# Larger projection sessions at block borders in an attention and mixture-of-experts kernel on one core

## The chip, the core and the metric

The kernel runs on one core of one Trainium2 chip. A core has five engines that run their own instruction streams and wait for each other by semaphores: TensorE (PE in the profile; its weight loads are shown apart as PEld), VectorE (DVE), ScalarE (ACT), GpSimd (POOL) and SyncE (SP, which here only issues DMAs). TensorE writes to PSUM, which has 8 banks of 512 fp32 columns on 128 partitions; DVE and ACT read PSUM and write SBUF. The metric is the device time of one execution in microseconds (us), the median of several runs. Lower is better.

## What is computed

```python
def _attn_ref(x, state):                 # x (8,8,512,64), state (8,8,32,64)
    scores = scale * x @ state^T         # every token against 32 states
    xread  = softmax(scores) @ state
    scores2 = scale * state @ x^T
    sread  = softmax(scores2) @ x
    return concat([xread, sread], axis=2)

def _moe_ref(x, w_gate, w1, w2):         # x (4352, 512), 8 experts, F = 1024
    P = exp(x @ w_gate - max); 8 rounds of row and column normalisation
    for e in range(E):
        out += P[:, e:e+1] * (maximum(x @ w1[e], 0) @ w2[e])
```

The rows of the second part are, for each of 8 batches, the 512 token rows of xread and the 32 state rows of sread, with 8 heads of 64 side by side.

## The kernel before

The first 141 us hold the attention, the gate with its normalisation rounds and expert 0. They are ordered by a small planner (`issue`, `op`) and are not touched by the change, apart from a variable that is dropped. The rest, experts 1 to 7, is written out by one loop (L871 to L894), and its order of issue is the order of execution on each engine.

The loop runs over (e, bi): expert e, and block bi of 9. Blocks 0 to 7 are the 512 token rows of a batch; block 8 (`bi == B`) is the **state block**, the 256 state rows of all batches. For each (e, bi) two layers are needed, and layer 1 of the next block is interleaved with layer 2 of this one.

**The projection** (`project`, L192 to L208). Since xread is softmax times state, x @ w1 is computed as softmax times (state @ w1). V = state @ w1 of one block is a tile of 2 pair groups by 1024 columns, made in two **halves** of 512 columns. A half is 8 small matmuls with 64 rows and 32 columns of the array each (`tile_position`), into two PSUM banks (q = 0, 1), and two ACT copies from them to V. A run of such matmuls without others between them is called a **session** here. Before, a session makes both halves of block work[i + 2], right after the first product of block i, and takes four banks of the pool with tag "h". State blocks have no projection, so the sessions stand in blocks 0 to 5, 7 and 8 of an expert. There are three V tiles.

**Layer 1** (`layer1`, L227 to L249) makes the hidden rows. One step makes one of 8 **hidden groups**: matmuls into a bank `hps` of pool "h" (4 banks in turn; two matmuls of 512 columns for a token block, four of 256 for the state block), and a relu on ACT into `Hm`. After the 4th and the 8th step DVE makes a set of four sums and differences from four relu results (L245 to L248, tile `sm` and a part of `Hm` in place). They are for the fast multiplication scheme with 7 products instead of 8.

**Layer 2** (`layer2`, L279 to L342) has the 7 **products**, k = 0 to 6. Each is 8 matmuls of 256 columns (4 in the state block) into one bank: A, E, B, A, B, E, B, where A and E are pools of one bank and B is one of two seed banks `Bseed`, used in turn by block number. After product 0 ACT copies A to the B bank, so that the further products add to it. After each of the products 1 to 6 DVE adds the bank, weighted by the routing column, to `acc` in two instructions (L307; one in the state block). A product into a bank waits for the add that read it.

**The interleaving** (L880 to L887). After product k follow so many steps of layer 1 as the pattern (0, 0, 1, 2, 2, 2, 1) says for k. `step()` is called after every product and every step of layer 1, 15 times a block; each sixth call advances the weight loader `load_w` (L160), which first issues the four weight DMAs of the next expert on POOL's queue, later makes eight DVE subtractions from w2 (tile `T`, L178). What is left of it is done at the end of block 6 (L891). In expert 1 POOL also scales `acc` by the first routing column (`weigh`, L251).

The last block has its own second layer (`layer2_last`).

Of the kernel before, what the change touches and what calls it, by code (L numbers as in the profile page):

```python
# [9 lines left out]
FP32 = mybir.dt.float32  # L10
FP16 = mybir.dt.float16
AX_X = mybir.AxisListType.X
ALU = mybir.AluOpType
AF = mybir.ActivationFunctionType
EPS = 1e-9


class Ring:
# [71 lines left out]
def kernel(  # L90
# [9 lines left out]
    nc = tc.nc  # L100

    B, H, S, D = x.shape
    Ns = state.shape[2]
    Dm, E = moe_w_gate.shape
    F = moe_w1.shape[2]
# [7 lines left out]
    NQ = NP // 2  # L113
# [19 lines left out]
    def bank(shape, dtype, name, tag="bank"):  # L133
        return pools[tag].tile(shape, dtype, name=name, tag=tag)
# [23 lines left out]
    vpool = ctx.enter_context(tc.tile_pool(name="vpool", bufs=3))  # L158
# [24 lines left out]
    w16 = [None] * E  # L183
# [5 lines left out]
    asb = actx.enter_context(tc.tile_pool(name="attn_sb", bufs=2))  # L189
    spl = actx.enter_context(tc.tile_pool(name="stprep", bufs=1))  # L190

    def project(e, bi):  # L192
        if bi == B:
            return
        w1h = w16[e][0]
        V = vpool.tile([128, NQ, F], FP16, name="V", tag="V")
        vt[(e, bi)] = V
        for f in range(F // 512):
            cols = ds(f * 512, 512)
            ps = [bank([128, 512], FP32, "v_ps", ring[0]) for _ in range(NQ)]  # L200
            for j in range(4):
                for q in range(NQ):
                    r = ((j ^ q) % 2) * 64
                    nc.tensor.matmul(ps[q][ds(j * Ns, Ns), :], stT[ds(r, 64), bi, q, ds((j ^ q) * Ns, Ns)],  # L204
                                     w1h[ds(r, 64), 2 * q + j // 2, cols],
                                     tile_position=(r, j * Ns))
            for q in range(NQ):
                nc.scalar.copy(out=V[:, q, cols], in_=ps[q])  # L208

    def hidden_ps(e, bi, fb, out):  # L210
        w1h = w16[e][0]
# [7 lines left out]
            nc.tensor.matmul(out, lhs, rhs, start=(k == 0), stop=(k == len(terms) - 1))  # L219

    vt = {}
    ring = ["bank"]
    hid = {}
    final = (E - 1, B)
    seeds = []

    def layer1(e, bi):  # L227

        t0, tn = blocks[bi]
        th = tn // 2  # L230
        Hm = hpool.tile([128, 2, NJ, S], FP16, name="Hm", tag="Hm")
        sm = hpool.tile([128, 3, NJ, S // 2], FP16, name="sm", tag="sm")
        hid[(e, bi)] = (Hm, sm)
        for j in range(NJ):
            for i in range(2):
                fb = i * NJ + j
                hps = bank([128, S], FP32, "hps", "h")
                hidden_ps(e, bi, fb, hps[:, :tn])
                nc.scalar.activation(out=Hm[:, i, j, :tn], in_=hps[:, :tn], func=AF.Relu)  # L239
                if j % 2 and i and (e, bi) != final:  # L240
                    jj = ds(j - 1, 2)
                    a11, a21 = Hm[:, 0, jj, :th], Hm[:, 0, jj, th:tn]
                    a12, a22 = Hm[:, 1, jj, :th], Hm[:, 1, jj, th:tn]
                    s1, s2, s4 = (sm[:, k, jj, :th] for k in range(3))
                    nc.vector.tensor_add(s1, a21, a22)  # L245
                    nc.vector.tensor_sub(a21, a11, a21)  # L246
                    nc.vector.tensor_sub(s2, s1, a11)  # L247
                    nc.vector.tensor_sub(s4, a12, s2)  # L248
                yield  # L249

    def weigh(b):  # L251
# [27 lines left out]
    def layer2(e, bi, n):  # L279
        t0, tn = blocks[bi]  # L280
        nk = tn // 256
        th = tn // 2
        Hm, sm = hid.pop((e, bi))
        w2h, T = w16[e][1], tsum[e]
        tb = t0 // 128
        p = Pmat[:, :, e:e + 1]
        A = bank([128, 2, DH], FP32, "A", "A")
        Eb = bank([128, 2, DH], FP32, "E", "E")

        def product(dst, lhs, rhs, first=False):  # L290
            for c in range(nk):
                for j in range(NJ):
                    nc.tensor.matmul(dst[:, c], lhs(j, c), rhs[:, j],  # L293
                                     start=first and c == 0 and j == 0, stop=(j == NJ - 1),
                                     skip_group_check=True)

        def h(i, half):
            return lambda j, c: Hm[:, i, j, ds(half * th + c * 128, 128)]

        def s(k):  # L300
            return lambda j, c: sm[:, k, j, ds(c * 128, 128)]

        def add(src, row, col):
            for c in range(nk):
                k = tb + row * nk + c
                dst = acc[:, k, ds(col * DH, DH)]
                nc.vector.scalar_tensor_tensor(out=dst, in0=src[:, c], scalar=p[:, k], in1=dst,  # L307
                                               op0=ALU.mult, op1=ALU.add)

        if e == 1:  # L310
            for b in range(2) if bi == 0 else (bi + 1,):
                weigh(b)
        product(A, h(0, 0), w2h[:, :NJ, :DH], True)
        if not n:
            for i in range(2):
                bb = pb.tile([128, 2, DH], FP32, name="Bseed%d" % i)
                nc.tensor.matmul(bb.rearrange("p c d -> p (c d)"), identh, aT[:, 0, 0], start=True, stop=True)
                seeds.append(bb)
        Bb = seeds[n % 2]
        nc.scalar.copy(out=Bb[:, :nk], in_=A[:, :nk])  # L320
        yield
        product(Eb, s(0), T[:, 0], True)
        add(Eb, 1, 1)
        yield
        product(Bb, s(1), T[:, 1])
        add(Bb, 0, 1)
        yield
        product(A, h(1, 0), w2h[:, NJ:, :DH])
        add(A, 0, 0)
        yield  # L330
        product(Bb, h(0, 1), T[:, 2])
        add(Bb, 1, 1)
        yield
        product(Eb, s(2), w2h[:, NJ:, DH:])
        add(Eb, 0, 1)
        yield
        product(Bb, h(1, 1), T[:, 3])
        add(Bb, 1, 0)
        if e == E - 1 and bi < B:
            for k in range(2 * nk):  # L340
                nc.sync.dma_start(out=outx[bi][:, k, :], in_=acc[:, tb + k, :])
        yield  # L342
# [44 lines left out]
    for g in range(2):  # L387
# [10 lines left out]
        out=wg_st, in_=moe_w_gate.rearrange("(kc p) e -> p kc e", p=128)))  # L398
# [28 lines left out]
    for g in range(4):  # L427
        ps = psum([128, 4, 128], FP16, "stT_ps")
# [13 lines left out]
    def gmul(_):  # L442
        for b in range(B):
            for j in range(4):
                for q in range(NQ):
# [6 lines left out]
                  lambda eng, q=q: copy(eng, G[:, :, q], gps[q].tile), [gm_op], uses=[gps[q]])  # L452
# [33 lines left out]
    for b in range(B):  # L486
        xT = slot(axt, 3, [128, H * NSC // 2, 128], FP16, "xT")
        xt_ready = []
        for g in range(2 if b < NT else 0):
            ps = psum([128, 8, 128], FP16, "xT_ps")  # L490
# [19 lines left out]
        for q in range(NQ):  # L510
            r = lambda n, b=b, q=q: (due_x(2 * b + q) + 0.1 * 5.54 * n,)
            ps = Slot(rings["pair"], lambda: bank([128, 2, 512], FP32, "psB", "pair"))
# [69 lines left out]
            s1 = op(r(4), {"DVE": (0.60, 0.80)}, subA, [m1], [], [eA, mxA])  # L582
# [71 lines left out]
    def tile_of(tag, shape):  # L654
# [4 lines left out]
    c = sk({"DVE": (0.36, 0.48)}, lambda: nc.vector.reduce_max(  # L659
        out=tile_of("lmx", [128, 1]), in_=logits.rearrange("p t e -> p (t e)"), axis=AX_X), gates)  # L660
    mT = psum([1, 128], FP32, "mT_ps")
    c = sk({"PE": (0.11, 0.35)}, lambda: nc.tensor.transpose(mT.tile, sm_["lmx"], ident32), [c, make32], takes=[mT])
    c = sk({"DVE": (0.25, 0.40)}, lambda: nc.vector.tensor_reduce(
        out=tile_of("gm", [1, 1]), in_=mT.tile, op=ALU.max, axis=AX_X, negate=True), [c], uses=[mT])
# [77 lines left out]
    for bi in range(len(blocks)):  # L742
        t0, tn = blocks[bi]
# [64 lines left out]
    for bi in range(2):  # L808
# [14 lines left out]
        for j in range(NJ):  # L823
# [11 lines left out]
            if j % 2:  # L835
                def sums(_, bi=bi, jj=ds(j - 1, 2), th=th, tn=tn):
                    Hm, sm = hid[1, bi]
                    a11, a21 = Hm[:, 0, jj, :th], Hm[:, 0, jj, th:tn]
                    a12, a22 = Hm[:, 1, jj, :th], Hm[:, 1, jj, th:tn]
                    s1, s2, s4 = (sm[:, k, jj, :th] for k in range(3))  # L840
                    nc.vector.tensor_add(s1, a21, a22)
                    nc.vector.tensor_sub(a21, a11, a21)
                    nc.vector.tensor_sub(s2, s1, a11)
                    nc.vector.tensor_sub(s4, a12, s2)
# [11 lines left out]
    for tag in ("A", "E"):  # L856
        pools[tag] = ctx.enter_context(
            tc.tile_pool(name="psum_" + tag, bufs=1, space=bass.MemoryType.PSUM))
    ring[0] = "h"
    n = 0  # L860

    def step():
# [6 lines left out]
                wload.pop(0)  # L869

    work = [(e, bi) for e in range(1, E) for bi in range(len(blocks))]  # L871
    for i, (e, bi) in enumerate(work):
        if bi == 1 and e + 1 < E:
            wload.append(load_w(e + 1))
        if (e, bi) == final:
            layer2_last()
            break
        l2 = layer2(e, bi, i)
        l1 = layer1(*work[i + 1]) if i + 1 < len(work) and work[i + 1] not in hid else iter(())
        for k in range(7):  # L880
            next(l2)
            step()
            if k == 0 and i + 2 < len(work) and work[i + 2] not in vt:
                project(*work[i + 2])
            for _ in range((0, 0, 1, 2, 2, 2, 1)[k]):
                next(l1, None)
                step()  # L887
        for part in (l1, l2):
            for _ in part:
                pass  # L890
        if bi == len(blocks) - 3:  # L891
            for _ in (x for w in wload for x in w):
                pass
            wload.clear()  # L894
# [30 lines left out]
```

## Time and profile before

| | |
|---|---|
| median of three runs | 766.16 us (766.08 to 768.02) |
| the profiled execution | 765.04 us |
| its span in the trace | 763.3 us |
| instructions | 16286 |
| experts 1 to 7, first product to last hidden group | 141.98 to 755.66 us |
| projection matmuls in them (L204) | 864, in 54 sessions |
| relu of layer 1 on ACT (L239) | 496, 572 ns each |
| copies of V on ACT (L208) | 216, 608 ns each |
| adds to acc on DVE (L307) | 708, 478 ns each |

A row of a view has the engine, the line of the kernel, the operation, the tile written and the tiles read, the shape and the count, then times in us. In a time line the first number is the start from the beginning of the span, the second the duration from the first start to the last end of the merged instructions; in square brackets stands how long the engine had been idle and which engine's work ended that. Consecutive matmuls overlap in these rows, since each is shown until its result is written: what a group costs is read from one start to the next.

### The profile page before, as it was taken

To read this page: it belongs to the slowest core of one execution; us is meant where nothing else is said; L and a number is where in the kernel's file an instruction comes from. 1 tells how busy PE (TensorE), PEld (TensorE's weight loads), DVE (VectorE), ACT (ScalarE), POOL (GpSimd) and SP (SyncE) were. 2 spreads that over 40 slices of the span, in tenths; PEclk is the share of its full clock that TensorE was granted. 3 is DMA by queue.
4 is the path that set the end of the run, shared out by engine and by line. 5 is a ranking of instruction groups with operands and counts; after the bars stand their busy time and mean duration, and the time that the engine had idled before them with its cause. 6 is when DMAs were issued, how large, how long until landed. Compare 5 with 4: busy or idle time off the path is not lost.

```text
span 763.3 us, 16286 instructions
## 1 busy us (share of the span) xinstructions
PE 747.2 (98%) x6557; PEld 501.5 (66%) x6557; DVE 626.8 (82%) x1533; ACT 513.3 (67%) x1002; POOL 104.5 (14%) x102
## 2 busy tenths in 40 slices
PE   5999999999999999999999999999999999999997
PEld 3444445566776667766776666766677666767676
DVE  6998977888987888888897888888887888878885
ACT  5888976666667675766657665676656666576652
POOL 4433100799200000100001000000001000000000
PEclk9999999999999999999999999999999999999999
DMA  8997200060015000510006000240006000002334
GB/s 135 190 147 123 46 1 1 1 112 1 1 24 89 1 2 1 88 25 2 1 1 111 2 1 1 38 75 1 1 2 101 11 2 1 1 34 85 104 111 139
DMA packets 41595, 34.61 MB, mean 45 GB/s; under 512 B 16688, under 2 KB 33072, under 8 KB 41520
## 3 DMA queue, kind: packets, MB, share of 16 engines
q0 software_dynamic: 21248, 20.97, 17.7%
q1 hardware_dynamic: 19040, 12.08, 6.0%
q8 instruction: 51, 0.84, 0.5%
q10 hardware_dynamic: 1232, 0.52, 0.3%
q14 instruction: 24, 0.20, 0.1%
HBM read 42.48 MB, written 8.91 MB: 67 GB/s over the span
## 4 chain that ended last, share of the span: by engine, by line
PE 91%; DVE 5%; ACT 3%; DMA 1%; issue 0%
PE hps L219 27%; PE Bseed L293 20%; PE E L293 14%; PE A L293 13%; PE yps L769 7%; PE v_ps L204 4%; PE hps L734 4%; DVE acc L307 1%; DVE sm L245 1%; ACT Hm L239 1%; PE su_ps L609 1%; DMA st_st<-in_state_dram 1%; ACT V L370 1%; PE y L271 0%; PE v_ps L712 0%; ACT xT L370 0%
## 5 line engine op out<-in xcount | busy, mean ns | idle before, releaser
L239 ACT ACTIVATE Hm<-hps 128x512 f16<-128x512 f32 (+1 forms) x496 | 266.1, 572 | 188.4 <-PE hps L219 173.4
L219 PE MATMUL hps<-aT,V 128*128 128x512 f16 x880 | 234.9, 379 | 0.0
L293 PEld LDWEIGHTS <-Hm 128*128 128x128 f16 x1888 | 184.6, 98 | 68.9 <-ACT Hm L376 0.3
L307 DVE SCALAR_TENSOR_TENSOR acc<-Bseed,Pmat,acc 128x256 f32<-128x256 f32 x354 | 155.4, 478 | 56.6 <-PE Bseed L293 54.1
L293 PEld LDWEIGHTS <-sm 128*128 128x128 f16 x1416 | 133.1, 98 | 51.8 <-DVE sm L245 23.8
L293 PE MATMUL A<-w2h,Hm 128*128 128x256 f16 x944 | 123.5, 273 | 0.0
L293 PE MATMUL Bseed<-T,Hm 128*128 128x256 f16 x944 | 123.3, 273 | 0.0
L219 PEld LDWEIGHTS <-V 128*128 128x128 f16 x880 | 86.1, 98 | 45.2
L208 ACT CAST V<-v_ps 128x512 f16<-128x512 f32 x216 | 111.2, 608 | 0.0
L307 DVE SCALAR_TENSOR_TENSOR acc<-E,Pmat,acc 128x256 f32<-128x256 f32 x236 | 103.3, 477 | 4.5 <-PE E L293 0.9
L245 DVE TENSOR_TENSOR sm<-Hm 128x512 f16<-128x512 f16 (+1 forms) x122 | 51.1, 419 | 19.3 <-ACT Hm L239 18.5
L769 PE MATMUL yps<-w2h,hT 128*128 128x512 f16 x272 | 66.5, 380 | 0.0
L307 DVE SCALAR_TENSOR_TENSOR acc<-A,Pmat,acc 128x256 f32<-128x256 f32 x118 | 51.9, 479 | 15.8 <-PE A L293 15.7
L293 PE MATMUL E<-T,sm 128*128 128x256 f16 x472 | 63.7, 274 | 0.6
L293 PE MATMUL Bseed<-T,sm 128*128 128x256 f16 x472 | 61.8, 273 | 0.0
L293 PE MATMUL E<-w2h,sm 128*128 128x256 f16 x472 | 61.7, 273 | 0.0
L255 POOL TENSOR_SCALAR acc<-acc,Pmat 128x512 f32<-128x512 f32 x34 | 55.2, 1638 | 44.8 <-DVE Pmat L686 44.8
L166 POOL DMA_DIRECT2D w1h<-in_moe_w_dram x12 | 8.6, 720 | 355.2 <-PE hps L219 355.2
L248 DVE TENSOR_TENSOR sm<-Hm,sm 128x512 f16<-128x512 f16 (+1 forms) x122 | 52.5, 430 | 4.2
L246 DVE TENSOR_TENSOR Hm<-Hm 128x512 f16<-128x512 f16 (+1 forms) x122 | 51.0, 418 | 4.2
L247 DVE TENSOR_TENSOR sm<-sm,Hm 128x512 f16<-128x512 f16 (+1 forms) x122 | 49.4, 405 | 0.0
L320 ACT COPY Bseed<-A 128x512 f32<-128x512 f32 (+1 forms) x62 | 34.1, 549 | 18.7 <-PE A L293 17.2
(110 smaller groups left out, 561.6 us busy)
## 6 DMA issues: line engine op xcount, KB each, us to landing
w1h<-in_moe_w_dram POOLq DMA_DIRECT2D x16, 512.0 KB, 7.1
w2h<-in_moe_w_dram POOLq DMA_DIRECT2D x16, 512.0 KB, 7.7
out_dram<-acc SPq DMA_DIRECT2D x32, 256.0 KB, 2.8
x_nat<-in_x_dram POOLq DMA_DIRECT2D x16, 256.0 KB, 5.9
st_st<-in_state_dram SPq DMA_DIRECT2D x1, 256.0 KB, 4.5
st_st<-in_state_dram ACTq DMA_DIRECT2D x1, 256.0 KB, 4.9
out_dram<-acc SPq DMA_DIRECT2D x4, 64.0 KB, 1.7
out_dram<-acc ACTq DMA_DIRECT2D x4, 64.0 KB, 2.0
```

The costliest lines, as they stand in the source:

```text
L208: nc.scalar.copy(out=V[:, q, cols], in_=ps[q])
L219: nc.tensor.matmul(out, lhs, rhs, start=(k == 0), stop=(k == len(terms) - 1))
L239: nc.scalar.activation(out=Hm[:, i, j, :tn], in_=hps[:, :tn], func=AF.Relu)
L245: nc.vector.tensor_add(s1, a21, a22)
L246: nc.vector.tensor_sub(a21, a11, a21)
L247: nc.vector.tensor_sub(s2, s1, a11)
L248: nc.vector.tensor_sub(s4, a12, s2)
L255: nc.gpsimd.tensor_scalar(out=acc[:, k, :], in0=acc[:, k, :], scalar1=Pmat[:, k, 0:1], scalar2=None, op0=ALU.mult)
L293: nc.tensor.matmul(dst[:, c], lhs(j, c), rhs[:, j], start=first and c == 0 and j == 0, stop=(j == NJ - 1), skip_group_check=True)
L307: nc.vector.scalar_tensor_tensor(out=dst, in0=src[:, c], scalar=p[:, k], in1=dst, op0=ALU.mult, op1=ALU.add)
L320: nc.scalar.copy(out=Bb[:, :nk], in_=A[:, :nk])
L769: nc.tensor.matmul(yps.tile, hT[fb].tile[:, ds(tk * 128, 128)], w2h[:, fb, :], start=(fb == 0), stop=(fb == NFB - 1))
```

## The change

The loop no longer projects block work[i + 2] after product 0 of block i. All halves of experts 1 to 7 that are still to be made stand in one list in the order of need, and a session takes the next few of them at the start of block i, before product 0. `SESS` names the blocks that have one and its size: three halves in blocks 7, 0, 2, 3 and 5, one half in block 6, none in blocks 1, 4 and 8; the very first session has two. Of three halves the first goes to the E bank and to the seed bank of this block, the other two to the four "h" banks. The copies of the first half are issued on ACT before product 0, those of the last two after ACT's copy of A to the seed bank.

The pattern of layer 1's steps depends on the block: `PATV` with a session, `PAT0` without, `PATS` in the state block, `PATN` in block 7 of the last expert, which has no half left to make. None has a step after product 6. While the state block runs, layer 1 of the next expert's block 0 is interleaved; its first set of sums is held back (`late`) and issued after the next product and its add. The variable `ring` is dropped.

```diff
@@ -13,6 +13,11 @@
 ALU = mybir.AluOpType
 AF = mybir.ActivationFunctionType
 EPS = 1e-9
+SESS = {7: 3, 0: 3, 2: 3, 3: 3, 5: 3, 6: 1}
+PATV = (0, 0, 1, 3, 2, 2, 0)
+PAT0 = (0, 1, 1, 2, 2, 2, 0)
+PATS = (1, 1, 1, 1, 2, 2, 0)
+PATN = (1, 1, 1, 2, 2, 1, 0)
 
 
 class Ring:
@@ -189,23 +194,30 @@
     asb = actx.enter_context(tc.tile_pool(name="attn_sb", bufs=2))
     spl = actx.enter_context(tc.tile_pool(name="stprep", bufs=1))
 
-    def project(e, bi):
-        if bi == B:
-            return
-        w1h = w16[e][0]
-        V = vpool.tile([128, NQ, F], FP16, name="V", tag="V")
-        vt[(e, bi)] = V
-        for f in range(F // 512):
+    def project(halves, n):
+        banks = []
+        for k, (e, bi, f) in enumerate(halves, 3 - len(halves)):
+            if (e, bi) not in vt:
+                vt[(e, bi)] = vpool.tile([128, NQ, F], FP16, name="V", tag="V")
+            w1h = w16[e][0]
             cols = ds(f * 512, 512)
-            ps = [bank([128, 512], FP32, "v_ps", ring[0]) for _ in range(NQ)]
+            if k:
+                ps = [bank([128, 512], FP32, "v_ps", "h") for _ in range(NQ)]
+            else:
+                ps = [bank([128, 512], FP32, "v_ps", "E"), seeds[n % 2].rearrange("p c d -> p (c d)")]
             for j in range(4):
                 for q in range(NQ):
                     r = ((j ^ q) % 2) * 64
                     nc.tensor.matmul(ps[q][ds(j * Ns, Ns), :], stT[ds(r, 64), bi, q, ds((j ^ q) * Ns, Ns)],
                                      w1h[ds(r, 64), 2 * q + j // 2, cols],
                                      tile_position=(r, j * Ns))
-            for q in range(NQ):
-                nc.scalar.copy(out=V[:, q, cols], in_=ps[q])
+            banks.append([(vt[(e, bi)][:, q, cols], ps[q]) for q in range(NQ)])
+        for dst, src in sum(banks[:-2], []):
+            nc.scalar.copy(out=dst, in_=src)
+        yield
+        for dst, src in sum(banks[-2:], []):
+            nc.scalar.copy(out=dst, in_=src)
+        yield
 
     def hidden_ps(e, bi, fb, out):
         w1h = w16[e][0]
@@ -219,8 +231,8 @@
             nc.tensor.matmul(out, lhs, rhs, start=(k == 0), stop=(k == len(terms) - 1))
 
     vt = {}
-    ring = ["bank"]
     hid = {}
+    late = []
     final = (E - 1, B)
     seeds = []
 
@@ -238,14 +250,19 @@
                 hidden_ps(e, bi, fb, hps[:, :tn])
                 nc.scalar.activation(out=Hm[:, i, j, :tn], in_=hps[:, :tn], func=AF.Relu)
                 if j % 2 and i and (e, bi) != final:
-                    jj = ds(j - 1, 2)
-                    a11, a21 = Hm[:, 0, jj, :th], Hm[:, 0, jj, th:tn]
-                    a12, a22 = Hm[:, 1, jj, :th], Hm[:, 1, jj, th:tn]
-                    s1, s2, s4 = (sm[:, k, jj, :th] for k in range(3))
-                    nc.vector.tensor_add(s1, a21, a22)
-                    nc.vector.tensor_sub(a21, a11, a21)
-                    nc.vector.tensor_sub(s2, s1, a11)
-                    nc.vector.tensor_sub(s4, a12, s2)
+                    def sums(jj=ds(j - 1, 2)):
+                        a11, a21 = Hm[:, 0, jj, :th], Hm[:, 0, jj, th:tn]
+                        a12, a22 = Hm[:, 1, jj, :th], Hm[:, 1, jj, th:tn]
+                        s1, s2, s4 = (sm[:, k, jj, :th] for k in range(3))
+                        nc.vector.tensor_add(s1, a21, a22)
+                        nc.vector.tensor_sub(a21, a11, a21)
+                        nc.vector.tensor_sub(s2, s1, a11)
+                        nc.vector.tensor_sub(s4, a12, s2)
+
+                    if bi == 0 and j == 1:
+                        late.append(sums)
+                    else:
+                        sums()
                 yield
 
     def weigh(b):
@@ -856,7 +873,6 @@
     for tag in ("A", "E"):
         pools[tag] = ctx.enter_context(
             tc.tile_pool(name="psum_" + tag, bufs=1, space=bass.MemoryType.PSUM))
-    ring[0] = "h"
     n = 0
 
     def step():
@@ -869,20 +885,29 @@
                 wload.pop(0)
 
     work = [(e, bi) for e in range(1, E) for bi in range(len(blocks))]
+    halves = [(e, bi, f) for e, bi in work if bi < B and (e, bi) not in vt for f in range(F // 512)]
     for i, (e, bi) in enumerate(work):
         if bi == 1 and e + 1 < E:
             wload.append(load_w(e + 1))
         if (e, bi) == final:
             layer2_last()
             break
+        v, pat = iter(()), PATS if bi == B else PATN if bi == B - 1 else PAT0
+        if bi in SESS and halves:
+            some = SESS[bi] if i else F // 512
+            v, pat = project(halves[:some], i), PATV
+            del halves[:some]
+        next(v, None)
         l2 = layer2(e, bi, i)
         l1 = layer1(*work[i + 1]) if i + 1 < len(work) and work[i + 1] not in hid else iter(())
         for k in range(7):
             next(l2)
             step()
-            if k == 0 and i + 2 < len(work) and work[i + 2] not in vt:
-                project(*work[i + 2])
-            for _ in range((0, 0, 1, 2, 2, 2, 1)[k]):
+            if k == 0:
+                next(v, None)
+            if late:
+                late.pop()()
+            for _ in range(pat[k]):
                 next(l1, None)
                 step()
         for part in (l1, l2):
```

## The prediction

> **What bounds the kernel now.** I read the page first, then TensorE's time line over whole blocks, then the waits of TensorE's weight loads, then the DVE and ACT rows of the blocks that looked different. The page:
>
> ```profile
> span 763.3 us, 16286 instructions
> PE 747.2 (98%) x6557; PEld 501.5 (66%) x6557; DVE 626.8 (82%) x1533; ACT 513.3 (67%) x1002; POOL 104.5 (14%) x102
> PEclk9999999999999999999999999999999999999999
> PE 91%; DVE 5%; ACT 3%; DMA 1%; issue 0%
> ```
>
> TensorE is the bound and its clock is full. A change can only win where TensorE doesn't stream. One ordinary block with a projection session, and one without (first column start, second duration, us):
>
> ```profile
> 408.69 1.04 PE L293 MATMUL A<-w2h,Hm 128*128 128x256 f16 x8
> 409.65 0.63 PE L204 MATMUL v_ps<-w1h,stT 64*32 64x512 f16 x16
> 410.21 1.05 PE L293 MATMUL E<-T,sm 128*128 128x256 f16 x8
> 411.09 1.04 PE L293 MATMUL Bseed<-T,sm 128*128 128x256 f16 x8
> 411.97 0.59 PE L219 MATMUL hps<-aT,V 128*128 128x512 f16 x2
> 412.40 1.04 PE L293 MATMUL A<-w2h,Hm 128*128 128x256 f16 x8
> ...
> 418.92 1.04 PE L293 MATMUL A<-w2h,Hm 128*128 128x256 f16 x8
> ...
> 736.02 1.04 PE L293 MATMUL A<-w2h,Hm 128*128 128x256 f16 x8
> 736.85 0.42 DVE L245 TENSOR_TENSOR sm<-Hm 128x512 f16<-128x512 f16 x1 [0.18 <-ACT Hm L239]
> 736.89 1.27 PE L293 MATMUL E<-T,sm 128*128 128x256 f16 x8
> 737.14 0.57 ACT L320 COPY Bseed<-A 128x512 f32<-128x512 f32 x1 [0.32 <-PE A L293]
> 738.00 1.04 PE L293 MATMUL Bseed<-T,sm 128*128 128x256 f16 x8
> ...
> 745.82 1.04 PE L293 MATMUL A<-w2h,Hm 128*128 128x256 f16 x8
> ```
>
> Starts, not durations, tell the price, because matmuls are pipelined. A product of 8 matmuls takes 0.87 (412.40 less 411.97 and 0.43 for a hidden group before it; 736.89 less 736.02). The session costs 410.21 - 408.69 - 0.87 = 0.65 for 2 halves of 8 small matmuls. A session block is 10.23, one without is 9.80. In the latter the E product takes 738.00 - 736.89 = 1.11, 0.24 too long: its third matmul needs the second set of sums, whose first instruction began at 736.85. In a session block the session covers that wait.
>
> ```profile
> PEld L293 <- DVE sm L245: 23.8, 60, 0.4
> PEld L204 <- issue: 11.6, 54, 0.4
> ```
>
> 54 sessions; the first row's waits fall mostly under sessions and cost nothing there. So outside its matmuls TensorE loses little: the entries and exits of 54 sessions, and 0.24 in each block without one (block 6 of seven experts, block 7 of the last: 8).
>
> **The change, part by part.** I count on blocks bi of 9, products k = 0 to 6 (A, E, B, A, B, E, B), t from a block's first TensorE instruction.
>
> *Fewer sessions.* A pass of 8 small matmuls on 8 separate tiles streams 512 columns, as one hidden matmul does: 0.43/2 = 0.22. So 0.65 is 2 x 0.22 + 0.21 of entry and exit. I take 0.23 for a third pass (a little over its stream), so 0.88 for three halves, 0.42 for one. 108 halves were 54 x 0.65 = 35.1. Now: 33 sessions of 3, 7 of 1 (bi 6), 1 of 2 (the first) = 29.0 + 2.9 + 0.65 = 32.6. **Gain 2.5.** No row has a third pass in one session: its price lies between 0.22 and 0.33 (0.65 for two), so the gain lies between 2.8 and -0.8.
>
> In the Trainium skill, "TensorEngine Tiling (Array Packing)", section Key Properties, it is the change of tiling mode, and not of tile, that drains TensorE. By that rule a third pass pays no drain, and the sum stays as it is; nothing in this trace separates the two.
>
> *The last hidden group moved ahead of product 6* (all four patterns end in 0). The relu and sums of the last group now run under product 6, 0.87, more than the 0.24 that was missing: **gain 1.9** (8 x 0.24). In the new blocks without session the sums' first instruction ends about 0.45 after the border and is needed at 0.87 + 0.22. Cover gone, it would cost up to 0.24 again in each.
>
> *What is free.* ACT copies as many V halves as before. The two extra banks are copied while A runs, and freed about 1.1 after the session starts (E is wanted at 1.75). The four h banks are asked for after the border, when the last relu is done. The second seed bank was last read two blocks ago. No DMA is moved; a block still has 15 steps of the weight loader, so its subtractions stay within the same blocks.
>
> *Two hand-overs without slack.* They need these rows:
>
> ```profile
> 415.01 1.03 PE L219 MATMUL hps<-aT,V 128*128 128x512 f16 x4
> 415.64 1.08 ACT L239 ACTIVATE Hm<-hps 128x512 f16<-128x512 f32 x2 [0.65 <-PE hps L219]
> 416.27 0.43 DVE L245 TENSOR_TENSOR sm<-Hm 128x512 f16<-128x512 f16 x1 [0.19 <-ACT Hm L239]
> 417.87 0.87 DVE L307 SCALAR_TENSOR_TENSOR acc<-E,Pmat,acc 128x256 f32<-128x256 f32 x2
> 418.69 0.88 DVE L307 SCALAR_TENSOR_TENSOR acc<-Bseed,Pmat,acc 128x256 f32<-128x256 f32 x2
> ...
> 420.03 0.57 ACT L320 COPY Bseed<-A 128x512 f32<-128x512 f32 x1 [0.32 <-PE A L293]
> ...
> 484.46 0.87 DVE L307 SCALAR_TENSOR_TENSOR acc<-Bseed,Pmat,acc 128x256 f32<-128x256 f32 x2
> 485.38 1.03 PE L293 MATMUL Bseed<-T,Hm 128*128 128x256 f16 x8
> ```
>
> The last two show that a B product waits for the add that read the same bank, and starts 0.05 after it (484.46 + 0.87 = 485.33).
>
> First, the copy of A into Bseed starts 1.11 after A (420.03 - 418.92), takes 0.57, plus 0.05: 1.73. With the session moved ahead of A, B(k=2) follows A and E directly: 1.75. Slack 0.02.
>
> Second, the fourth hidden group now comes at k=3, so the first set of sums is queued on DVE *before* the add of B(k=4), and product B(k=6) needs that add. From the start of the three hidden groups at k=3: relus start at 0.63, 1.12, 1.61 (415.64 - 415.01; 1.08 for two against 0.60 for one); the last ends at 2.21; sums start at 2.24 and take 1.60 (416.27 to 417.87); add B 3.84 to 4.71; B(k=6) may start at 4.76. TensorE gets there after 1.30 + 4 x 0.87 = 4.78. Slack 0.02; 0.07 in blocks without session, where the groups come in twos. This concerns 35 session blocks. A neighbouring wait that takes the place of the slack can be worth -0.05 to +0.15 each; I take 0.01 for each, as every duration in it is measured: **loss 0.4** (0 to 5).
>
> *Sums under POOL.* While POOL scales acc (137 to 196 us, expert 1, bi 0 to 4) DVE's sums are slower. The first four rows are from 144 to 195 us, the fifth from the whole trace:
>
> ```profile
> L248 DVE TENSOR_TENSOR sm<-Hm,sm 128x512 f16<-128x512 f16 x9 | 6.1, 676 | 0.3
> L245 DVE TENSOR_TENSOR sm<-Hm 128x512 f16<-128x512 f16 x9 | 4.8, 535 | 0.9 <-ACT Hm L239 0.9
> L246 DVE TENSOR_TENSOR Hm<-Hm 128x512 f16<-128x512 f16 x9 | 4.6, 511 | 0.3
> L247 DVE TENSOR_TENSOR sm<-sm,Hm 128x512 f16<-128x512 f16 x9 | 3.8, 417 | 0.0
> L255 POOL TENSOR_SCALAR acc<-acc,Pmat 128x512 f32<-128x512 f32 x34 | 55.2, 1638 | 44.8 <-DVE Pmat L686 44.8
> ```
>
> A set is 0.68 + 0.54 + 0.51 + 0.42 = 2.14 there against some 1.69 elsewhere (4 x 0.42): 0.45 longer. Before, nothing stood behind it; now B(k=6) does, without slack: **loss 2.1** (5 x 0.45 less 2 x 0.07; between 0 if the sums miss POOL, and 4.1 if each is as slow as this one, 0.88 + 0.43 + 0.42 + 0.79 = 2.52):
>
> ```profile
> 150.25 0.88 DVE L245 TENSOR_TENSOR sm<-Hm 128x512 f16<-128x512 f16 x1 [0.18 <-ACT Hm L239]
> ...
> 151.96 0.79 DVE L248 TENSOR_TENSOR sm<-Hm,sm 128x512 f16<-128x512 f16 x1
> ```
>
> In the Trainium skill, "SBUF — State Buffer", section Who interferes with whom, an instruction of DVE with two SBUF inputs contends with a GpSimd instruction that reads SBUF, and whoever comes second is blocked for the other's whole instruction. The trace agrees that there is contention, but a set is lengthened by 0.45 on average, not by POOL's 1.64.
>
> *The session waits for the E bank.* The add of E(k=5) ends 0.87 after 4.66 (add B and then 0.82), + 0.05 = 5.58; the session's first matmul is at 4.78 + 0.87 + 0.09 (409.65 - 408.69 - 0.87) = 5.74. Slack 0.16. In bi 6 of experts 2, 4, 6 the loader's step falls between the two adds and puts one subtraction there:
>
> ```profile
> 482.33 0.75 DVE L178 TENSOR_TENSOR T<-w2h 128x512 f16<-128x512 f16 x2
> ```
>
> 0.33 (0.75 less 0.42), so bi 7's session, and product A behind it, start 0.17 late: 3 x 0.17 = **0.5**. At the state block every product has 4 matmuls (0.44). There four products and four hidden groups come first (8 x 0.435 = 3.48), so add B(k=4) starts at 3.48 + 0.44 + 0.2 = 4.12 and holds DVE to 4.5; the sums that were put off to it run to 6.1, add E to 6.6; with 0.05 that is 0.04 past the next session's 6.62 (15 groups x 0.435 + 0.09): 6 x 0.04 = **0.2**. Were the sums not put off, add B would end at 6.4 and B(k=6) be late by 0.35. The state block itself has no session now, and its loss of cover costs nothing as the last sums come before its border.
>
> *Sum against the profiled execution* (765.04, which is its span 763.3 and 1.7 around it): 2.5 + 1.9 - 0.4 - 2.1 - 0.5 - 0.2 = 1.2 gained, so 763.8. Its median of three runs is 766.16, 1.1 above it; on that scale **764.9**.
>
> **The rivals.**
>
> *The slow sums stay off the path.* POOL's phase against DVE moves with the new order, or the add finds another gap. For it: the clean sets leave 0.02 to 0.07, and the lengthening is one or two instructions of a set; against: all nine sets in that stretch average 2.14. Without the 2.1: 762.8.
>
> *The hand-overs decide (slower).* The place is B(k=2) and B(k=6) of the 35 session blocks. Slack of 0.02 is within what two rounded starts can hide, and any further delay on ACT or DVE is passed on at once. At 0.15 a block it is 5.3 in place of 0.4: 764.9 + 4.9 = 769.8. From 0.11 a block (3.9 against 1.6 of other gain) it is slower by over 2.3. Against it: the durations repeat to 0.01 in the blocks shown.
>
> *The sessions get no cheaper.* If a third pass costs 0.33, the 2.5 turns to -0.8: 768.2; at 0.30, no gain by sessions, 767.4. Entry and exit are then a price of each half. For it: no row shows a third pass; against: 0.65 for two passes of 0.22 leaves 0.09 ahead of the first, a place that only an entry has.
>
> *The lock holds for a whole POOL instruction.* 5 x 1.64 in place of 2.1: 771.0. Nine sets speak against it.
>
> **How the numbers follow.** About 0.3% (2.3 us) is what a measurement of this kernel can tell from no change. Forecast 764.9, 0.42, own range 763.4 to 766.4: of it 0.12 faster, 0.30 within. Slow sums off the path 0.26, faster. Hand-overs 0.20: slower 0.17, within 0.03. Sessions no cheaper 0.10: within 0.08, slower 0.02. Lock 0.02, slower. Together faster 0.38, within 0.41, slower 0.21. The range goes from 762.4 (the second case with the 0.4 of hand-overs given back) to 769.4, which leaves out the worst of the hand-overs and the lock.
>
> **What would show it.** In the changed trace: three-half sessions 0.88 from the last start before to the first after; sessions of about 41; E after A at 0.87 in every block without session; B(k=6) late by 0.3 to 0.8 in expert 1's first five blocks with the wait on DVE's acc add, and at most 0.05 late after; ACT's Bseed copy named before B(k=2) only for hundredths. I am wrong if waits of TensorE on acc adds or on the Bseed copy are seen in most session blocks, or if none is seen before 196 us.

## The result and the profile after

| | before | after |
|---|---|---|
| median of 22 runs each | 766.04 us (764.77 to 768.53) | 764.19 us (762.81 to 767.4) |
| ratio after to before | | 0.9978, 95% interval 0.9968 to 0.9987 |
| the profiled execution | 765.04 us | 765.52 us |

The change makes the kernel about 1.7 us faster (0.0022 x 766), against 1.2 forecast: within 0.3%, as the likeliest case had it. The profiled execution of the kernel after does not show it in its span:

```profile
span 763.7 us, 16205 instructions
PE 742.7 (97%) x6557; PEld 505.4 (66%) x6557; DVE 620.0 (81%) x1533; ACT 510.5 (67%) x1002; POOL 104.9 (14%) x102
```

The reason is in the part that the change doesn't touch. These are the last hidden matmuls ahead of the loop over experts 1 to 7 and the first of the last layer, in the kernel before and then after:

```profile
141.33 0.81 PE L734 MATMUL hps<-aT,V 128*128 128x512 f16 x3
...
755.66 3.64 PE L271 MATMUL y<-w2h,Hm 128*128 128x512 f16 x24
```

```profile
143.60 0.81 PE L751 MATMUL hps<-aT,V 128*128 128x512 f16 x3
...
756.14 3.64 PE L288 MATMUL y<-w2h,Hm 128*128 128x512 f16 x24
```

The last hidden group (the last two of the three matmuls, 0.22 after the row's start) begins at 141.55 before and at 143.82 after, so this execution came to the loop 2.3 us later. From there to the first product of the last layer, **the loop's length**, it is 755.66 - 141.55 = 614.11 before and 756.14 - 143.82 = 612.32 after: 1.79 gained, as the timed runs have it. Below each kernel is compared by this length from its own profile, read in the same way. Of a time line only the rows that a reading needs are shown.

The border with a three-half session, then one with a one-half session, TensorE alone. The first row is product B(k=6) of the block ahead, and A is the first product of the new block:

```profile
217.55 1.03 PE L310 MATMUL Bseed<-T,Hm 128*128 128x256 f16 x8
218.52 0.39 PE L211 MATMUL v_ps<-w1h,stT 64*32 64x512 f16 x1
...
218.74 0.62 PE L211 MATMUL v_ps<-w1h,stT 64*32 64x512 f16 x16
219.29 0.83 PE L310 MATMUL A<-w2h,Hm 128*128 128x256 f16 x6
```

```profile
207.54 1.04 PE L310 MATMUL Bseed<-T,Hm 128*128 128x256 f16 x8
208.50 0.41 PE L211 MATMUL v_ps<-w1h,stT 64*32 64x512 f16 x8
208.85 1.05 PE L310 MATMUL A<-w2h,Hm 128*128 128x256 f16 x8
```

Three halves cost 219.29 - 217.55 - 0.87 = 0.87, one half 208.85 - 207.54 - 0.87 = 0.44. Two were 0.65. So a half costs 0.22, its stream alone, and a session 0.22 once. A block without a session:

```profile
276.35 1.04 PE L310 MATMUL A<-w2h,Hm 128*128 128x256 f16 x8
277.22 1.04 PE L310 MATMUL E<-T,sm 128*128 128x256 f16 x8
278.09 0.59 PE L231 MATMUL hps<-aT,V 128*128 128x512 f16 x2
```

E takes 0.87 here (278.09 - 277.22), as in every block without a session: the wait of 0.24 for the sums is gone. What came in its place, in expert 1 (rows of POOL, DVE and TensorE):

```profile
152.44 5.24 POOL L272 TENSOR_SCALAR acc<-acc,Pmat 128x512 f32<-128x512 f32 x3
152.84 0.80 DVE L258 TENSOR_TENSOR Hm<-Hm 128x512 f16<-128x512 f16 x1
153.56 0.41 DVE L259 TENSOR_TENSOR sm<-sm,Hm 128x512 f16<-128x512 f16 x1
...
154.04 1.03 PE L231 MATMUL hps<-aT,V 128*128 128x512 f16 x4
154.35 0.87 DVE L324 SCALAR_TENSOR_TENSOR acc<-Bseed,Pmat,acc 128x256 f32<-128x256 f32 x2
...
155.27 1.03 PE L310 MATMUL Bseed<-T,Hm 128*128 128x256 f16 x8 [0.20 <-DVE acc L324]
```

One of the sums takes 0.80 in place of 0.42. The add of B(k=4) comes after them and ends at 154.35 + 0.87 = 155.22, and product B(k=6) starts 0.05 later, at 155.27. It was due at 154.04 + 0.87 = 154.91: 0.36 late. Read in the same way, the five first blocks are late by 0.36, 0.45, 0.28, 0.79 and 0.30, 2.2 in all. Where POOL is done the same chain just fits:

```profile
294.55 0.87 DVE L324 SCALAR_TENSOR_TENSOR acc<-Bseed,Pmat,acc 128x256 f32<-128x256 f32 x2
294.62 1.03 PE L231 MATMUL hps<-aT,V 128*128 128x512 f16 x4
295.49 1.04 PE L310 MATMUL Bseed<-T,Hm 128*128 128x256 f16 x8
```

The add ends at 295.42, and the product starts on time, 0.87 after its hidden groups. The session that finds a weight subtraction (L183) ahead of the add to E, in block 7 of expert 2:

```profile
305.35 0.42 DVE L183 TENSOR_TENSOR T<-w2h,T 128x512 f16<-128x512 f16 x1
305.50 1.04 PE L310 MATMUL Bseed<-T,Hm 128*128 128x256 f16 x8
305.68 0.87 DVE L324 SCALAR_TENSOR_TENSOR acc<-E,Pmat,acc 128x256 f32<-128x256 f32 x2
...
306.61 0.37 PE L211 MATMUL v_ps<-w1h,stT 64*32 64x512 f16 x1
```

Without a wait it would start at 305.50 + 0.87 + 0.09 = 306.46: 0.15 late, in three experts. The session behind a state block, whose products take 0.44:

```profile
234.98 0.60 PE L310 MATMUL Bseed<-T,Hm 128*128 128x256 f16 x4
...
235.54 0.37 PE L211 MATMUL v_ps<-w1h,stT 64*32 64x512 f16 x1
```

It was due at 234.98 + 0.44 + 0.09 = 235.51: 0.03 late, in six experts. And the very first session:

```profile
145.21 0.62 PE L211 MATMUL v_ps<-w1h,stT 64*32 64x512 f16 x16 [0.80 <-ACT Hm L393]
145.77 1.05 PE L310 MATMUL A<-w2h,Hm 128*128 128x256 f16 x8
...
147.09 0.38 PE L310 MATMUL E<-T,sm 128*128 128x256 f16 x2
```

It waits for relus of the last hidden groups, whose banks it takes over, and product A stands behind it. E starts 147.09 - 143.82 = 3.27 after the last hidden group; before it was 144.10 - 141.55 = 2.55. That is 0.72 lost once.

### The profile page after: what moved, and what is told of

It is laid out like the page before. It is cut to its first block, busy times and chain, and to the rows that moved or that the text cites. A ratio compares the mean times of both kernels' runs of the same rounds, so it can differ in the third digit from the quotient of the medians.

```text
span 763.7 us, 16205 instructions
## 1 busy us (share of the span) xinstructions
PE 742.7 (97%) x6557; PEld 505.4 (66%) x6557; DVE 620.0 (81%) x1533; ACT 510.5 (67%) x1002; POOL 104.9 (14%) x102
## 4 chain that ended last, share of the span: by engine, by line
PE 76%; DVE 3%; ACT 2%; issue 0%
PE hps L231 25%; PE Bseed L310 19%; PE A L310 14%; PE E L310 13%; PE v_ps L211 4%; ACT Hm L251 2%; DVE acc L324 1%; DVE sm L260 1%; DVE Hm L258 1%; DVE sm L257 1%; PE y L288 0%; DVE sm L259 0%; DVE T L183 0%; PE Bseed L211 0%; DVE acc L290 0%
## 5 line engine op out<-in xcount | busy, mean ns | idle before, releaser
L231 PE MATMUL hps<-aT,V 128*128 128x512 f16 x880 | 230.2, 380 | 0.0
L310 PEld LDWEIGHTS <-Hm 128*128 128x128 f16 x1888 | 181.3, 98 | 73.3 <-issue 18.1
L310 PEld LDWEIGHTS <-sm 128*128 128x128 f16 x1416 | 138.3, 98 | 33.8
L219 ACT CAST V<-v_ps 128x512 f16<-128x512 f32 x150 | 77.7, 611 | 0.0
L310 PE MATMUL E<-T,sm 128*128 128x256 f16 x472 | 61.7, 273 | 0.0
```

Of the source, the lines that this page charges most:

```text
L219: nc.scalar.copy(out=dst, in_=src)
L310: nc.tensor.matmul(dst[:, c], lhs(j, c), rhs[:, j], start=first and c == 0 and j == 0, stop=(j == NJ - 1), skip_group_check=True)
```

## The experiments

Each is a small edit of the kernel after, or of the kernel before where its name begins with b. The ratio is to the kernel before, the length is the loop's.

| run | ratio, 95% interval | median, us | loop's length, us | against its base |
|---|---|---|---|---|
| a_noweigh | 0.9936 (0.9914 to 0.9958) | 761.13 | 610.12 | -2.20 |
| b_noweigh | 0.9994 (0.9978 to 1.001) | 765.2 | 613.86 | -0.25 |
| a_nolate | 0.9993 (0.9977 to 1.0008) | 765.74 | 614.25 | +1.93 |
| a_sess2 | 1.0008 (0.9989 to 1.0026) | 767.03 | 615.55 | +3.23 |
| a_extra | one execution | 763.76 | 612.31 | -0.01 |
| a_extra_behind | one execution | 779.38 | 625.25 | +12.93 |
| b_pat | 0.9998 (0.9987 to 1.0009) | 765.93 | 613.78 | -0.33 |
| b_pat_ahead | 0.9966 (0.9953 to 0.9978) | 763.8 | 612.13 | -1.98 |
| a_split | 0.9937 (0.9919 to 0.9955) | 761.46 | 609.56 | -2.76 |
| a_split_first | 0.9919 (0.9901 to 0.9936) | 759.93 | 609.03 | -0.53 (to a_split) |

### The scaling on POOL left out, after and before

```diff
         if e == 1:
-            for b in range(2) if bi == 0 else (bi + 1,):
-                weigh(b)
+            pass
```

> The changed kernel without POOL's scaling of acc by the first routing column (the scaling is left out, so expert 0's part is added unweighted). Theory: in expert 1's first five blocks the sums on DVE are stretched by POOL, the add of B(k=4) stands behind them, and product B(k=6) waits 0.28 to 0.79 us for it, 2.2 us in all. Without the scaling these five waits vanish, sums in that stretch take 0.42 each as elsewhere, and the time falls by 2.2 against the changed kernel (ratio to the kernel before about 0.995). Rival: the five waits come from something else in expert 1 (the first blocks after the planner, DMA); then they stay and the time does not move by more than 0.5.

> The kernel before, with the same scaling left out. Theory: there the add of B(k=4) stands ahead of the first set of sums, so stretched sums meet no waiting product: gain 0.1 to 0.3 (two small gaps of under 0.1 near 145 and 155 us), ratio 1.000 to 0.9995. Rival: POOL's stretch costs TensorE time in any order; then the gain is as large as in the changed kernel, 2 us.

The kernel after gains 2.20 in the loop, the kernel before 0.25. In the kernel after, the same place of the first block without POOL's work:

```profile
152.50 0.87 DVE L324 SCALAR_TENSOR_TENSOR acc<-Bseed,Pmat,acc 128x256 f32<-128x256 f32 x2
152.56 1.03 PE L231 MATMUL hps<-aT,V 128*128 128x512 f16 x4
153.43 1.04 PE L310 MATMUL Bseed<-T,Hm 128*128 128x256 f16 x8
```

The add ends at 153.37 and B(k=6) starts on time (152.56 + 0.87). No product of the loop is late by more than 0.02 in this kernel's trace. So the five waits are POOL's stretch of the sums, met by the new order: both are needed. The first rival (the slow sums stay off the path) has fallen.

### The state block's sums issued at once

```diff
-                    if bi == 0 and j == 1:
-                        late.append(sums)
-                    else:
-                        sums()
+                    sums()
```

> The changed kernel with the state block's first set of sums issued at once, not one product later. Theory: the set runs from 4.3 to 5.9 us of the state block, add B(k=4) ends at 6.4, and product B(k=6), due at 6.09, is 0.35 late: six state blocks, 2.0 us slower than the changed kernel. Rival: the state block has slack on DVE and the delay is hidden: no difference (within 0.5).

1.93 lost, as expected. In the state block of expert 1:

```profile
232.00 1.03 PE L231 MATMUL hps<-aT,V 128*128 128x512 f16 x4
...
232.69 0.48 DVE L321 SCALAR_TENSOR_TENSOR acc<-Bseed,Pmat,acc 128x256 f32<-128x256 f32 x1
...
233.22 0.60 PE L307 MATMUL Bseed<-T,Hm 128*128 128x256 f16 x4 [0.19 <-DVE acc L321]
```

The product waits for the add (232.69 + 0.48 + 0.05 = 233.22). It was due at 232.00 + 0.87 = 232.87: 0.35 late, in each of the six state blocks. Without the part that holds these sums back (`late`) the change would gain nothing.

### Sessions of two halves only

```diff
-SESS = {7: 3, 0: 3, 2: 3, 3: 3, 5: 3, 6: 1}
+SESS = {b: 2 for b in range(8)}
```

> The changed kernel with sessions of two halves at the border of blocks 0 to 7 and none of three: 54 sessions as before the change, at the new place, no use of the E and seed banks. Theory: what a session costs beyond its matmuls is 0.20 for entry and exit, once; 13 more sessions cost 2.7, less 0.6 for the waits for the E bank that go: 2.1 slower than the changed kernel; up to 2 more if hidden group 1 waits for the V copy of the same session. Rival (the price goes by halves, size is nothing): 0.6 faster than the changed kernel.

3.23 lost: 13 more sessions at 0.22 are 2.9, less 0.6 for the waits for the E bank that go. The rest, 0.9, is at a place that I had not named. After the state block:

```profile
235.00 1.09 ACT L251 ACTIVATE Hm<-hps 128x512 f16<-128x512 f32 x2 [0.21 <-PE hps L231]
235.23 0.60 PE L310 MATMUL Bseed<-T,Hm 128*128 128x256 f16 x4
235.76 0.78 PE L211 MATMUL v_ps<-w1h,stT 64*32 64x512 f16 x16
236.47 0.72 PE L310 MATMUL A<-w2h,Hm 128*128 128x256 f16 x5
```

The session's passes and exit take 236.47 - 235.76 = 0.71, where the first pass's start to the next product is 0.56 for two halves elsewhere (410.21 - 409.65 before): 0.15 within the session, after each of the six state blocks. The reading is that its second half takes the banks of the last two relus, which end at 235.00 + 1.09 = 236.09; with three halves the E and seed banks come first, and in the kernel after no such session is late by more than the 0.03 shown. The rival (the price goes by halves) has fallen.

### One more DVE instruction, ahead of the sums and behind them

```diff
+    spare = persist.tile([128, 512], FP16, name="spare")
...
+                if j == 1 and i and e > 1 and 0 < bi < B:
+                    nc.vector.tensor_sub(spare, aT[:, 0, 0], aT[:, 0, 1])
                 if j % 2 and i and (e, bi) != final:
```

and behind (the same spare tile):

```diff
                     else:
                         sums()
+                    if j == 1 and e > 1 and 0 < bi < B:
+                        nc.vector.tensor_sub(spare, aT[:, 0, 0], aT[:, 0, 1])
```

> The changed kernel with one more DVE subtraction of 128x512 fp16 into a spare tile ahead of the first set of sums, in token blocks of experts 2 to 7 (42 blocks). Theory: the chain relu, sums, add B(k=4), product B(k=6) has 0.02 us of slack in session blocks and 0.07 in the others, so some 0.34 of DVE work is passed on to TensorE: 30 x 0.32 + 12 x 0.27 = 12.8 us slower than the changed kernel. Rival: DVE is idle a fifth of the time and takes it without loss: under 1 us.

> The changed kernel with the spare DVE subtraction of 128x512 fp16 put behind the first set of sums instead of ahead of it, in the same 42 blocks. Ahead of the set it ran in DVE's wait for the relu. Theory: behind the set it stands between the sums and add B(k=4), a chain with 0.02 us of slack (0.07 in blocks without a session): product B(k=6) is 0.27 to 0.34 late in each, 12 us slower than the changed kernel over experts 2 to 7. Rival: the chain is not on TensorE's path outside expert 1: under 1 us.

Ahead of the sums it cost nothing, and my expectation was wrong, though not for the rival's reason alone: the instruction depends on nothing, so DVE ran it while it waited for the relu that the sums need. In a block of expert 2:

```profile
249.50 0.41 DVE L254 TENSOR_TENSOR spare<-aT 128x512 f16<-128x512 f16 x1
...
250.25 0.42 DVE L260 TENSOR_TENSOR sm<-Hm 128x512 f16<-128x512 f16 x1 [0.34 <-ACT Hm L252]
```

DVE is done with it at 249.91 and still idle for 0.34 before the sums. That place has cover; the chain begins at the relu. Behind the sums the same instruction cost 12.93, over 42 blocks 0.31 each:

```profile
254.46 0.43 DVE L261 TENSOR_TENSOR sm<-Hm,sm 128x512 f16<-128x512 f16 x1
254.80 0.42 DVE L268 TENSOR_TENSOR spare<-aT 128x512 f16<-128x512 f16 x1
254.93 1.03 PE L232 MATMUL hps<-aT,V 128*128 128x512 f16 x4
255.14 0.87 DVE L327 SCALAR_TENSOR_TENSOR acc<-Bseed,Pmat,acc 128x256 f32<-128x256 f32 x2
256.06 0.71 PE L313 MATMUL Bseed<-T,Hm 128*128 128x256 f16 x5
```

The spare instruction moves the add by 0.34 (255.14 - 254.80), and the product, due at 254.93 + 0.87 = 255.80, starts at 256.06, 0.05 after the add's end. DVE is busy 81% of the span, and yet 0.34 us of its work at this place costs as much on TensorE, less a slack of 0.02 to 0.07: in this trace the product is 0.32 to 0.33 late in the 30 blocks with a session and 0.27 in the 12 without.

### The move of the last steps alone, in the kernel before

```diff
-            for _ in range((0, 0, 1, 2, 2, 2, 1)[k]):
+            for _ in range((0, 1, 1, 2, 2, 2, 0)[k] if bi == B - 2 or (e == E - 1 and bi == B - 1) else (0, 0, 1, 2, 2, 2, 1)[k]):
```

> The kernel before, with one part of the change alone: in the 8 blocks without a projection session the steps of layer 1 go (0,1,1,2,2,2,0), so that none comes after product 6. Theory: the wait of 0.24 us in product E for the sums goes in each of them: 1.9 us faster than the kernel before (ratio 0.9975). Rival: the wait moves to another product of these blocks, and nothing is gained.

Nothing to speak of was gained: seven of the eight waits stayed. The sums that E waits for are made in the block ahead, so the edit was made one block too late; only the last expert's block 7 lost its wait, as the block ahead of it was edited too (the next expectation says that all eight stayed, which is one too many). Again, one block ahead:

```diff
-            for _ in range((0, 0, 1, 2, 2, 2, 1)[k]):
+            for _ in range((0, 0, 1, 3, 2, 2, 0)[k] if bi == B - 3 or (e == E - 1 and bi == B - 2) else (0, 0, 1, 2, 2, 2, 1)[k]):
```

> The kernel before with the steps (0,0,1,3,2,2,0) in the block ahead of each block without a session (block 5 of each expert, block 6 of the last). The sums for which product E waits are made in the block ahead of it, so the steps have to move there; moving them in the block itself left all eight waits. Theory: the eight waits of 0.24 us in product E go, 1.9 us faster than the kernel before (ratio 0.9975), in the trace the E products of these blocks take 0.87. Rival: with add B(k=4) now behind the first set of sums, product B(k=6) waits as long as E did: no gain.

1.98 gained; 8 x 0.24 is 1.9. In this kernel's block 6 of expert 1:

```profile
205.75 1.04 PE L293 MATMUL E<-T,sm 128*128 128x256 f16 x8
206.62 1.04 PE L293 MATMUL Bseed<-T,sm 128*128 128x256 f16 x8
```

E takes 0.87 here, and no other product is late in its place. This small part alone does as much as the whole change (ratios 0.9966 and 0.9978, with intervals that overlap). It touches 8 blocks, and POOL's scaling is over before the sums that it moves.

### The sums split, and the first session put back

```diff
                     def sums(jj=ds(j - 1, 2)):
...
                         nc.vector.tensor_sub(a21, a11, a21)
+                        yield
                         nc.vector.tensor_sub(s2, s1, a11)
...
-                    if bi == 0 and j == 1:
-                        late.append(sums)
+                    if j == 1:
+                        late.append(sums())
                     else:
-                        sums()
+                        list(sums())
...
             if late:
-                late.pop()()
+                if next(late[0], 0) == 0:
+                    late.pop()
```

> The changed kernel with the first set of sums of every block held back and split: two instructions after product 4 and its add, two after product 5 and its add. Theory: add B(k=4) no longer stands behind the sums, add E(k=5) only behind two: the five waits under POOL (2.2), the three for the E bank behind a weight subtraction (0.4) and the six after the state block (0.2) go: 2.8 us faster than the changed kernel, ratio to the kernel before 0.994. Rival: DVE's work is only moved, and add B(k=6) or product E of the next block waits instead: no gain.

2.76 gained. The place of the first block that was shown twice above, now with two of the sums after each product's add:

```profile
152.52 0.43 DVE L258 TENSOR_TENSOR Hm<-Hm 128x512 f16<-128x512 f16 x1
152.81 1.03 PE L231 MATMUL hps<-aT,V 128*128 128x512 f16 x4
153.02 0.87 DVE L325 SCALAR_TENSOR_TENSOR acc<-E,Pmat,acc 128x256 f32<-128x256 f32 x2
153.68 1.04 PE L311 MATMUL Bseed<-T,Hm 128*128 128x256 f16 x8
153.81 0.41 DVE L260 TENSOR_TENSOR sm<-sm,Hm 128x512 f16<-128x512 f16 x1
155.05 0.71 DVE L258 TENSOR_TENSOR Hm<-Hm 128x512 f16<-128x512 f16 x1
```

B(k=6) starts on time, 0.87 after 152.81. POOL still stretches a sum (0.71), but nothing on TensorE is late behind it. Besides the sessions' entries and exits, no start of TensorE in this kernel's loop is late by more than 0.02, but for the first session. That one:

```diff
-        next(v, None)
+        if i:
+            next(v, None)
...
             if k == 0:
-                next(v, None)
+                for _ in range(1 if i else 2):
+                    next(v, None)
```

> As the kernel with split sums, and the very first session is put back after product A of the first block. Theory: the first session at the border waits 0.95 us for the banks of expert 0's last relus while product A could run; with A first, product E comes 0.7 earlier: 0.6 faster than the kernel with split sums alone. Rival: product A waits for the same relus, no difference.

0.53 gained in the loop. With both edits the kernel takes 759.93, ratio 0.9919 (0.9901 to 0.9936): faster than the kernel before by 6.2 (0.0081 x 766, by the interval 4.9 to 7.6; 5.1 by the loops' lengths) and faster than the kernel after, by 3.3 in the loop (612.32 - 609.03) and by 4.5 by the two ratios.

## Why the prediction was right

All in us, from the traces; a minus is a gain.

| step of the prediction | forecast | measured |
|---|---|---|
| 13 fewer sessions | -2.5 | -2.9 (13 x 0.22) |
| last hidden group ahead of product 6 | -1.9 | -1.9 (b_pat_ahead -1.98) |
| sums under POOL | +2.1 | +2.2 (a_noweigh 2.20) |
| two hand-overs without slack | +0.4 | 0 |
| E bank behind a weight subtraction | +0.5 | +0.4 (3 x 0.15) |
| E bank after the state block | +0.2 | +0.2 (6 x 0.03) |
| first session ahead of product A | not in the sum | +0.7 |
| sum | -1.2 | -1.3 |
| loop's length | | -1.79 |

The likeliest case was right, and most of its terms were right one by one. So were the signs that it named: three-half sessions of 0.87, 41 sessions, E at 0.87 after A in every block without a session, and B(k=6) late by 0.28 to 0.79 in expert 1's first five blocks. The slack was worked out from starts in the trace as 0.02, or 0.07 without a session. In the trace after, no B(k=2) and no B(k=6) outside expert 1 is late by more than 0.02, so the rival of the hand-overs fell; a_extra_behind shows that the slack at B(k=6) is no more than forecast. The forecast that the slow sums would cost just what they are stretched by came out (2.1 against 2.2), since they are passed on without cover. In a_sess2, whose blocks stand elsewhere against POOL's work, the same five waits are 2.1 in all. More than half of what sessions and covers gained, 4.8, was eaten by this new wait and by the first session.

Three sizes were off. A third pass costs its stream and nothing more, 0.22, where I took 0.23: that is most of the 0.4 by which the gain from the sessions came out larger. The hand-overs cost nothing, where I allowed 0.4. And the first session is a term that I did not see: I said that the h banks are asked for when the last relu is done, which holds in the loop, where a product without hidden groups stands between; at the loop's start the last hidden group stands right ahead of the session. These errors of size cancel to within 0.1 (-0.4 - 0.4 + 0.7). That is luck: with any one of them alone the sum would have been off by a third or more.

0.5 of the loop's gain is in no row of the table (1.79 against 1.3). Some 0.25 of it are six waits under 0.1 that the trace before has in experts 1, 2, 4 and 6 and the trace after has not. Another 0.15 goes with the sessions: the product right behind one takes 0.88 and not 0.87 (411.09 - 410.21 in the kernel before), and there are 13 fewer. The last 0.1 stays open.

The rival of sessions that get no cheaper fell with a_sess2 and with the 0.87 and 0.44 of three halves and one. Its price was misreckoned: if entry and exit were a price of each half, one half would cost 0.33 and not the 0.42 in its sum, and the 108 halves would cost what they did before, so 767.4 and not 768.2. That a third pass costs its stream alone (0.87 - 0.65 = 0.22) agrees with what the Trainium skill, "TensorEngine Tiling (Array Packing)", section Key Properties, states of a change of tile within one mode. The rival of the lock that holds for a whole POOL instruction fell too: the five waits were 0.28 to 0.79, not 1.64, and in the rows above the sum at 153.56 takes its usual 0.41 within one POOL instruction that runs from 152.44 to 154.23.

## What to carry to other kernels

On an engine that is full, count starts: what a change can win are the places where the next start is late, and what it can lose are the chains it makes just fit. When an instruction is moved in an in-order queue, ask which instruction now stands behind it and which engine waits for that one: 0.34 us of work on an engine that is idle a fifth of the time cost nothing ahead of a set of four sums and 0.31 a block behind it. When a chain fits with hundredths, look for the stretch of the run in which its instructions are slower than elsewhere.

## What was not expected of the hardware

The part ahead of the loop is the same work on TensorE in every kernel here. Yet its last hidden group began anywhere between 141.14 and 144.70 us in the twelve profiles, while the loop's length answers to an edit: the loop of a_extra, whose added instruction is hidden, is as long as that of the kernel after to 0.01. In the profile of the kernel after, one wait of TensorE in that part was for a DMA:

```profile
PE psB L534 <- DMA xT<-x_nat: 2.8, 1, 2.8
```

Such waits, of 1.0 to 2.5 in all, stand there in five of the other profiles too, among them the two other late ones (143.50 and 144.70), and the six profiles with less came to the loop by 142.59. Most of the spread between executions of one kernel (764.77 to 768.53 before) can lie there; that was not tested by itself.
